# Loading x in 5 KB runs, attention by head halves, filter rows turned by VectorE, and loads paced by stores, in a gated mix of a long convolution and dilated attention

## The chip, the cores and the metric

One core of a Trainium2 chip. The metric is the time of one execution in device microseconds. With one core a run is called slow when it lies over 1.5% above the fastest of the same kernel. A ratio in this text is the mean time of one kernel's fast runs over that of the other's fast runs of the same rounds, so it is not quite the ratio of the medians that stand beside it.

## The reference, cut to what matters

S = 2048 tokens, D = 640 channels, bf16. Two branches are mixed by a gate per token.

```python
g = sigmoid((x * gate_w).sum(-1, keepdims=True))            # x is A_q
# a: short shift filter of k (4 taps), times v, then a long convolution, times q
kv = k_shift * v
y  = irfft(rfft(kv, 2*S) * rfft(ssm_k, 2*S))[:S] + kv * ssm_D
a  = x * y
# b: 32 heads of 20 channels; each token attends to 8 positions, 2 apart
q, k, v = x @ wqkv ;  b = softmax(q . k_gathered, masked) . v_gathered @ wo
return g * a + (1 - g) * b
```

## The kernel before

Tokens are worked on in 36 blocks of 57 queries and 64 keys, of even and odd tokens apart. x is loaded block by block (overlapping blocks, runs of one token row, 1.25 KB), transposed by TensorE, and a ScalarE copy writes each transposed block contiguously:

```python
def transposes(m):                                   # 18 times, two blocks each
    tr = ppv.tile([128, 8, 128], BF, name="trx", tag="trx")
    for dt in range(NDT):
        nc.tensor.transpose(tr[:, dt, :], xs(m)[:, 128*dt:128*dt+128], ident[:, :])
    nc.scalar.copy(xT[:, :, 128*m:128*m+128], tr[:, 0:NDT])
```

Then come the v projection (12 of 18 pairs of blocks; the other six during attention), the gate, and projections of q and k, whose rows are collected in a stage tile `stg` and sent by DMA into the score operands `kq`. Two stage tiles exist, so a projection waits until an earlier tile is sent. VectorE meanwhile makes the kv product. Attention is 24 steps: scores, exponential on ScalarE (`ET`), products with v (`O`), division on VectorE (`oS`). The output projection (`tr`, `oT`, `op`, `fin`, store to `b_scr`) of a third of the tokens runs among the steps of the next third. At the end of the eighth step all inputs of the convolution are asked for at once:

```python
if k == NT - 1:
    load_h(0)                                           # filter, runs of 128 bytes
    nc.sync.dma_start(G[:], ...)                        # constants, 2 MB
    for q in range(4):
        nc.sync.dma_start(kv[32*q:32*q+32], ...)        # 2.6 MB
    for g in range(1, NG):
        load_h(g)
```

The convolution follows: first transforms (`Am`), second (`Up`, `Hs`), inverse (`i`, `Cm`), by five groups of 16 channels, and a last inverse with the mixing and the stores.

The softmax here doesn't subtract the row's maximum and nothing guards it: scores larger than these inputs give would overflow.

Of the kernel before, what the change touches and what calls it, by code (L numbers as in the profile page):

```python
# [18 lines left out]
D = 640  # L19
# [10 lines left out]
PRE = 7  # L30
XW = 2 * NSB * KB
# [100 lines left out]
def kernel(  # L132
# [33 lines left out]
    Dz = p0.tile([128, 160], BF, name="Dz")  # L166
    g_nat = p0.tile([128, 16], F32, name="g_nat")
    omg = p0.tile([128, 16], F32, name="omg")

# [3 lines left out]
    xS = pA.tile([128, 4 * 2 * NSB * CB], BF, name="xS", tag="K0")  # L173
# [11 lines left out]
    pr = pB.tile([128, 4, 4 * D], BF, name="pr")  # L185
    v23 = pB.tile([128, 2, 4, D], BF, name="v23")
# [3 lines left out]

    def xs(m):
        return xS[:, m * D:(m + 1) * D]
# [5 lines left out]
    def load_x(m0, m1):  # L198
        for sub in range(2):
            for m in range(m0, m1):  # L200
                k0, k1 = (PRE if sub == 0 and m % 9 == 0 else 0), (KB - 2 if sub == 1 and m % 9 == 8 else KB)
                if (k0, k1) != (0, KB):
                    for i, n in split16(k1 - k0):
                        nc.sync.dma_start(xs(m)[KB * sub + k0 + i:KB * sub + k0 + i + n],
                                          raw(x2, xrow(2 * m + sub, k0 + i) * D, [[2 * D, n], [1, D]]))
            ms = [m for m in range(m0, m1) if not ((sub == 0 and m % 9 == 0) or (sub == 1 and m % 9 == 8))]
            a = ms[0]
            for b, nxt in zip(ms, ms[1:] + [-1]):
                if nxt != b + 1:
                    nc.sync.dma_start(xS[KB * sub:KB * sub + KB, a * D:(b + 1) * D].rearrange("p (m d) -> p m d", d=D),  # L210
                                      raw(x2, xrow(2 * a + sub, 0) * D, [[2 * D, KB], [4 * QB * D, b + 1 - a], [1, D]]))
                    a = nxt

    def load_w(w):
        nc.sync.dma_start(W[:, :, w, :], W3[:, :, w, :])

    kh = kvw[:, 0:19 * D].rearrange("p (t d) -> p t d", d=D)
    vns = [kvw[:, (19 + 4 * e) * D:(23 + 4 * e) * D].rearrange("p (t d) -> p t d", d=D) for e in range(2)] + [v23[:, 0], v23[:, 1]]

    def load_kv(c):  # L220
        if c == 0:
            nc.gpsimd.memset(kh[0:1, 0:3, :], 0.0)
            for p, n in ((1, 112), (113, 15)):
                nc.sync.dma_start(kh[p:p + n, 0:3, :], raw(k2, (16 * p - 3) * D, [[16 * D, n], [D, 3], [1, D]]))
        nc.sync.dma_start(kh[:, 3 + 4 * c:7 + 4 * c, :], raw(k2, 4 * c * D, [[16 * D, 128], [D, 4], [1, D]]))
        nc.sync.dma_start(vns[c], raw(v2, 4 * c * D, [[16 * D, 128], [D, 4], [1, D]]))

    nc.sync.dma_start(ident[:], ca["ident"].ap())
    for m in (0, 9):
        nc.gpsimd.memset(xs(m)[0:PRE], 0.0)  # L230
        nc.gpsimd.memset(xs(m + 8)[96:128], 0.0)
    load_x(0, 4); load_w(2); load_x(4, 9); load_x(9, 13)
# [3 lines left out]
    load_x(13, 18)  # L236
    load_kv(0)
    load_w(1); load_w(0)
    for c in range(1, 4):
        load_kv(c)  # L240
    nc.gpsimd.memset(Dz[:], 0.0)
    nc.gpsimd.tensor_copy(VW[:, :, :, DH], valid[:].unsqueeze(2).to_broadcast([128, 18, H]))
    for q in range(4):
        nc.gpsimd.dma_start(Dz[32 * q:32 * q + 1, :], A_ssm_D[160 * q:160 * q + 160].unsqueeze(0))
# [6 lines left out]
    def kv_gen():  # L251
        nc.vector.tensor_copy(wl[:], wraw[:].rearrange("p c j -> p j c"))
# [26 lines left out]
    def transposes(m):  # L279
        tr = ppv.tile([128, 8, 128], BF, name="trx", tag="trx")  # L280
        for dt in range(NDT):
            nc.tensor.transpose(tr[:, dt, :], xs(m)[:, 128 * dt:128 * dt + 128], ident[:, :])
        nc.scalar.copy(xT[:, :, 128 * m:128 * m + 128], tr[:, 0:NDT])

    def vproj_half(m, a, ps):
        for dt in range(NDT):
            nc.tensor.matmul(ps, lhsT=xT[:, dt, 128 * m:128 * m + 128], rhs=W[:, dt, 2, 320 * a:320 * a + 320],  # L287
                             start=(dt == 0), stop=(dt == NDT - 1))

    def vproj(m):  # L290
        ps = ppv.tile([128, 2, 512], F32, name="psv", tag="mm", bufs=3)
        for a in range(2):
            vproj_half(m, a, ps[:, a, 0:320])
        nc.scalar.copy(VW[:, m, :, 0:DH].rearrange("p (a h) d -> p a h d", a=2),
                       ps[:, :, 0:320].rearrange("p a (h d) -> p a h d", h=16))
# [38 lines left out]
    def feat_copies(e):  # L334
        for t in range(4):
            if e or t:
                for p in range(2):
                    ld.copy(kq[e][:, t, NSB * p:NSB * p + NSB], kq[0][:, 0, NSB * p:NSB * p + NSB], 800, eng="d")
                    ld.t["d"] += 600
                    yield  # L340
# [16 lines left out]
    def qk_send(ft, stg):  # L357
        for h in range(H):
# [10 lines left out]
    def qk_gen():  # L369
        for ft in range(NDT - 1):  # L370
            stg = new_stg()
            for c in range(5):
# [3 lines left out]
                for part in range(2):  # L376
                    qk_evac(stg, c, part, ps[:, part])
                if c < 4:
                    yield
            if ft == 2:  # L380
# [3 lines left out]
                for _ in feat_copies(1):  # L384
                    pass
            qk_send(ft, stg)
            yield

    def late_qk():
        stg = new_stg()  # L390
        for c in range(5):
            for part in range(2):
                ps = ppa.tile([128, 512], F32, name="pj2", tag="w", bufs=2)
                qk_part(NDT - 1, c, part, ps)
                qk_evac(stg, c, part, ps, eng="da"[part])
                if (c, part) == (4, 1):
                    qk_send(NDT - 1, stg)
                yield

    def late_v():  # L400
        for m in range(12, 18):
            for a in range(2):
                ps = ppa.tile([128, 512], F32, name="pv2", tag="w", bufs=2)
                vproj_half(m, a, ps[:, 0:320])
                ld.copy(VW[:, m, 16 * a:16 * a + 16, 0:DH], ps[:, 0:320].rearrange("p (h d) -> p h d", h=16), 320, eng="da"[a])
                yield
# [9 lines left out]
    def s1_gen(key, g):  # L416
        Am = p3.tile([128, 64, 4, IL], BF, name="Am", tag="Am", bufs=3)
        st[key] = Am
        for oc in range(4):
            ps = ps_tile("s1")  # L420
            psq = ps[:].rearrange("p a m -> p (a m)").rearrange("p (q l j) -> p q l j", q=4, l=4)
            for il in range(4):
                i = 4 * oc + il
                for qp in range(2):
                    rows = slice(64 * qp, 64 * qp + 64)
                    if key[0] == "h":
                        lhsT = h_lin[rows, IL * g + i].rearrange("p c n -> p (c n)")
                    else:
                        lhsT = kv[rows, :, :, IL * g + i].rearrange("p c n -> p (c n)")
                    nc.tensor.matmul(psq[:, 2 * qp:2 * qp + 2, il, :], lhsT=lhsT, rhs=F1b[rows, :], start=True, stop=True,  # L430
                                     tile_position=(64 * qp, 0), skip_group_check=True)
            ld.copy(Am[:, :, :, 4 * oc:4 * oc + 4], psq.rearrange("p q l j -> p j q l"), 1024)
# [56 lines left out]
    transposes(0)  # L489
    transposes(1)  # L490
    for m in range(12):
        vproj(m)
        transposes(m + 2)
        advance(kvg, 1)
    for m in range(14, 18):
        transposes(m)
    gate()
    feats(0)
    ld.t = dict(a=0.0, d=4000.0)
    qk = qk_gen(); fc = feat_copies(0)  # L500
    for k in range(20):
        advance(qk, 1)
        advance(kvg, 1)
        if k >= 3:
            advance(fc, 2)
        if k == 12:
            gate_end()
    while advance(kvg, 1):
        pass
# [6 lines left out]
    wo = pD.tile([128, NDT, D], BF, name="wo")  # L516
    nc.sync.dma_start(wo[:], B_wo.rearrange("(t p) n -> p t n", p=128))
# [8 lines left out]
    halves = [(gi, t, hf) for gi in range(NGI) for t in range(NT) for hf in range(2)]  # L526
# [48 lines left out]
    def op_tr(j):  # L575
# [4 lines left out]
        oT = pD.tile([128, NDT, 128], BF, name="oT", tag="oT", bufs=3)  # L580
# [11 lines left out]
    def op_half(j, hf):  # L592
# [8 lines left out]
        if hf == 1:  # L601
            op_store(j)

# [24 lines left out]
    def load_h(g):  # L628
        for q in range(4):
            for c in range(2):  # L630
                nc.gpsimd.dma_start(h_lin[32 * q:32 * q + 32, IL * g:IL * g + IL, c, :],  # L631
                                  raw(A_ssm_k, (160 * q + 80 * c + IL * g) * S, [[64, 32], [S, IL], [1, 64]]))

    def tap0(g):
        r = h_lin[:, IL * g:IL * g + IL, :, 0]
        nc.vector.tensor_tensor(r, r, Dz[:].rearrange("p (c i) -> p i c", c=2)[:, IL * g:IL * g + IL], ALU.add)

    opg = None
    lqk, lv = late_qk(), late_v()
    steps = [(gi, t) for gi in range(NGI) for t in range(NT)]  # L640
    scores(0)
    scores(1)
    for k in range(len(steps)):
        if k + 1 < len(steps):
            scores(2 * k + 2)
            scores(2 * k + 3)
        pv(2 * k)
        pv(2 * k + 1)
        gi, t = steps[k]
        if gi == 0:  # L650
            advance(lqk, (3, 3, 2, 2, 0, 0, 0, 0)[t])
            advance(lv, (0, 0, 1, 2, 3, 3, 3, 0)[t])
        if k == NT - 1:
            sC.close()
            pF = ctx.enter_context(tc.tile_pool(name="pF", bufs=1, side="left", reuse_waits="tile"))
            kv = pF.tile([128, 2, 64, 80], BF, name="kv")
            G = pF.tile([128, 32, 2, 128], BF, name="G")
            h_lin = pF.tile([128, 80, 2, 64], BF, name="h_lin", tag="hl")
            load_h(0)
            nc.sync.dma_start(G[:], cf["G"].ap().rearrange("p (a r b) -> p a r b", a=32, r=2))  # L660
            for q in range(4):
# [125 lines left out]
```

## Time and profile before

| | before |
|---|---|
| median of 3 runs | 337.01 us (336.86 to 339.55) |
| span of the profiled run, mean clock | 335.7 us, 0.813 |
| head (loads, projections, kv product) | to 98.5 |
| attention with output projection | to 208.5 |
| convolution up to the first inverse matmul | to 243.7 |
| other groups; last inverse and stores | to 310; to 335.7 |

The prediction shows the page, the chain and the windows. Of the groups (busy time, mean ns of one, idle time before), the copy of a transposed block:

```profile
L283 ACT COPY xT<-trx 128x640 bf16<-128x640 bf16 x18 | 12.1, 698 | 6.0 <-PE trx L282 6.0
```

And TensorE's waits in attention, 98.5 to 208.5 us (columns: total us, how often, longest; "issue" means that the profile shows nothing that was awaited; that TensorE then had no instruction is my reading, from the holes 128 matmuls apart and the 43 packets of 16 KB on the instruction queue, both in the prediction):

```profile
PE sc L539 <- issue: 8.9, 3, 5.4
...
PE O L561 <- issue: 4.9, 1, 4.9
...
PE sc L539 <- DMA kq<-stg: 1.9, 2, 1.0
...
PE tr L579 <- DVE fin L600: 0.5, 1, 0.5
```

Read it as a budget: with the 1.2 us of issue before `op`, 15 us of attention are, by that reading, waits for instructions, and waits for rows or for the store buffers are almost nothing.

### The profile page before, as it was taken

Reading aid. Unit: us, or ns where it says so; the run is one execution under the profiler, and the core shown is the slowest. Engines: PE = TensorE matmul, PEld = TensorE weight load, DVE = VectorE, ACT = ScalarE, POOL = GpSimd, SP = SyncE. Lnnn points to the kernel's source line nnn. Section 1 sums busy time; section 2 is a strip of 40 time slices with the busy share of each in tenths; the row PEclk is TensorE's granted clock in tenths of the full one; section 3 lists DMA queues with packets and bytes.
Section 4 is the critical chain, followed back from the end, with each engine's and each line's share of the span. In section 5 each row is a group of like instructions: output and inputs, shape, how many; then the busy total and the mean of one; then the engine's idle time right before and its main releaser. Section 6 shows DMA issues by size and latency. Waiting matters only on the chain.

```text
span 335.7 us, 12259 instructions
## 1 busy us (share of the span) xinstructions
PE 238.3 (71%) x5549; PEld 175.0 (52%) x5556; DVE 188.4 (56%) x279; ACT 168.8 (50%) x247; POOL 52.9 (16%) x81
## 2 busy tenths in 40 slices
PE   1399899969549978643969987536696969677330
PEld 1277545535315655432746765536595958676320
DVE  0106999099924433211545555524949697973982
ACT  1167845355304544321546632625749595963670
POOL 7700231000200006235930000000000000000132
PEclk9999999999757997555877999567778797985855
DMA  6999953655375235997531112995503131397065
GB/s 174 227 220 361 415 140 94 144 120 145 108 146 129 56 85 199 212 199 159 130 96 31 43 53 85 206 234 139 129 2 87 45 86 44 66 221 159 19 164 138
DMA packets 16017, 46.23 MB, mean 138 GB/s; under 512 B 3811, under 2 KB 10833, under 8 KB 13872
## 3 DMA queue, kind: packets, MB, share of 16 engines
q1 hardware_dynamic: 13196, 38.14, 46.5%
q0 software_dynamic: 2768, 7.32, 8.3%
q8 instruction: 43, 0.70, 0.9%
q14 instruction: 10, 0.07, 0.1%
HBM read 26.75 MB, written 7.87 MB: 103 GB/s over the span
## 4 chain that ended last, share of the span: by engine, by line
PE 35%; DVE 22%; DMA 13%; issue 12%; ACT 10%; SPq 5%; POOL 0%; DVEq 0%; ACTq 0%; POOLq 0%
PE i L482 8%; PE op L595 6%; DVE pr L256 6%; PE s L445 5%; DMA kq<-stg 5%; ACT Am L119 4%; PE O L561 3%; DVE pr L260 3%; PE sc L539 3%; DMA xS<-in_A_q_dram 3%; PE pj L349 3%; DMA kvw<-in_A_k_dram 3%; DVE kq L121 3%; SPq L363 2%; ACT Up L119 2%
## 5 line engine op out<-in xcount | busy, mean ns | idle before, releaser
L349 PE MATMUL pj<-xT,W 128*128 128x456 bf16 (+3 forms) x243 | 50.9, 366 | 8.4 <-ACT stg L119 7.7
L542 ACT ACTIVATE ET<-sc 128x684 bf16<-128x684 f32 x48 | 33.3, 740 | 30.9 <-PE sc L539 28.7
L349 PEld LDWEIGHTS <-W 128*128 128x128 bf16 x250 | 24.8, 101 | 32.8 <-issue 13.2
L119 ACT CAST stg<-pj 128x456 bf16<-128x456 f32 (+3 forms) x45 | 21.4, 531 | 35.0 <-PE pj L349 17.7
L445 PE MATMUL s<-Am,G 64*128 64x64 bf16 x1280 | 25.6, 201 | 15.9 <-issue 11.6
L631 POOL DMA_DIRECT2D h_lin<-in_A_ssm_k_dram x40 | 25.8, 650 | 56.0 <-PE sc L539 40.3
L482 PE MATMUL i<-M,Hs 128*128 128x128 bf16 x160 | 28.9, 276 | 6.4 <-DVE Hs L469 4.3
L445 PEld LDWEIGHTS <-G 64*128 64x128 bf16 x1280 | 23.7, 103 | 17.4 <-issue 15.6
L256 DVE TENSOR_TENSOR pr<-kvw,wl 128x2560 bf16<-128x2560 bf16 x16 | 22.9, 1487 | 16.9 <-DMA kvw<-in_A_k_dram 16.8
L119 ACT CAST Am<-s 128x1024 bf16<-128x1024 f32 x25 | 24.1, 1060 | 12.8 <-PE s L430 8.4
L755 POOL DMA_DIRECT2D out_dram<-qg x12 | 6.0, 502 | 154.6 <-DVE qg L753 154.6
L482 PE MATMUL i<-M,Hw 128*128 128x128 bf16 x160 | 28.6, 276 | 0.4 <-DVE Hw L469 0.4
L595 PE MATMUL op<-wo,oT 128*128 128x320 bf16 x120 | 25.4, 359 | 3.8 <-ACT oT L582 2.3
L539 PE MATMUL sc<-kq 31*64 31x57 bf16 x1152 | 16.9, 206 | 14.6 <-issue 8.9
L482 PEld LDWEIGHTS <-Hs 128*128 128x128 bf16 x160 | 24.1, 159 | 5.1 <-DVE Hs L469 4.7
L568 DVE RECIPROCAL rd<-O 128x24 f32<-128x24 f32 x24 | 7.4, 306 | 34.5 <-PE O L561 34.5
L287 PEld LDWEIGHTS <-xT 128*128 128x128 bf16 x180 | 18.3, 105 | 14.1 <-issue 5.7
L539 PEld LDWEIGHTS <-kq 31*64 31x64 bf16 x1152 | 13.3, 115 | 22.9 <-issue 19.6
L482 PEld LDWEIGHTS <-Hw 128*128 128x128 bf16 x160 | 23.8, 158 | 2.6 <-DVE Am L121 1.1
L287 PE MATMUL psv<-W,xT 128*128 128x320 bf16 x120 | 20.8, 326 | 5.1 <-DMA W<-in_B_wqkv_dram 5.1
L119 ACT CAST Cm<-i 128x1024 bf16<-128x1024 f32 x13 | 13.1, 1012 | 19.7 <-PE i L482 19.7
L582 ACT COPY oT<-tr 128x640 bf16<-128x640 bf16 x18 | 12.5, 692 | 20.0 <-PE tr L579 19.7
(69 smaller groups left out, 409.9 us busy)
## 6 DMA issues: line engine op xcount, KB each, us to landing
Hw<-Hs SPq DMA_DIRECT2D x10, 512.0 KB
kq<-stg SPq DMA_DIRECT2D x28, 170.2 KB
kvw<-in_A_k_dram SPq DMA_DIRECT2D x4, 640.0 KB
kv_scr<-kvo POOLq DMA_DIRECT2D x4, 640.0 KB, 5.5
kv<-kv_scr SPq DMA_DIRECT2D x4, 640.0 KB
h_lin<-in_A_ssm_k_dram POOLq DMA_DIRECT2D x40, 64.0 KB, 4.0
qg<-in_A_q_dram SPq DMA_DIRECT2D x4, 640.0 KB
bl<-b_scr SPq DMA_DIRECT2D x4, 640.0 KB
```

Of the source, the lines that this page charges most:

```text
L119: self.nc.scalar.copy(dst, src)
L121: self.nc.vector.tensor_copy(dst, src)
L256: nc.vector.tensor_tensor(pr[:, j].rearrange("p (n c) -> p n c", n=4), kh[:, 4 * c + 3 - j:4 * c + 7 - j, :], wl[:, j, :].unsqueeze(1).to_ ...
L287: nc.tensor.matmul(ps, lhsT=xT[:, dt, 128 * m:128 * m + 128], rhs=W[:, dt, 2, 320 * a:320 * a + 320], start=(dt == 0), stop=(dt == NDT - 1))
L349: nc.tensor.matmul(ps[:, 0:nb * wd], lhsT=W[:, dt, which, 128 * ft:128 * ft + 128], rhs=rhs, start=(dt == 0), stop=(dt == NDT - 1))
L445: nc.tensor.matmul(o, lhsT=G[rows, j, r, :], rhs=Am[rows, 2 * j + r, :, :], start=(r == 0), stop=(r == 1), tile_position=(64 * c, 0), skip ...
L482: nc.tensor.matmul(o, lhsT=src[:, c, :, :, 8 * oc + il].rearrange("p q j -> p (q j)"), rhs=M[:, k, :], start=(k == 0), stop=(k == 1), skip ...
L539: nc.tensor.matmul(sc[64 * sub:64 * sub + 64, hh, QB * mb:QB * mb + QB], lhsT=kqt[r:r + DH + NF, t % 4, si, 0:KB], rhs=kqt[r:r + DH + NF, ...
L542: nc.scalar.activation(ETs[i % NET][:, :, 0:NW], sc[:, :, 0:NW], ACT.Exp, scale=SCALE)
L582: nc.scalar.copy(oT[:], tr[:])
L595: nc.tensor.matmul(op[:, 0:320], lhsT=oTs[j][:, ft, :], rhs=wo[:, ft, 320 * hf:320 * hf + 320], start=(ft == 0), stop=(ft == NDT - 1))
L631: nc.gpsimd.dma_start(h_lin[32 * q:32 * q + 32, IL * g:IL * g + IL, c, :], raw(A_ssm_k, (160 * q + 80 * c + IL * g) * S, [[64, 32], [S, IL ...
```

## The change

Its intent: fewer and longer DMA runs for x, with the overlapping key blocks cut out on the chip; attention ordered by halves of the heads, so that half of the staged rows may be sent later; the filter loaded in 4 KB rows and turned by 20 VectorE transposes; kv and G cut in eight pieces, one behind each of the first stores of output rows, instead of a flood; and two groups of the filter's first transform moved into attention. All 18 pairs of blocks of the v projection now precede attention, and the transposed output rows (`oT`) get two buffers instead of three. The diff, cut to its core:

```diff
-    def load_x(m0, m1):  ... blocks of 64 rows, 1.25 KB runs
+    def load_x(c):
+        nc.sync.dma_start(xN[:, 4*c:4*c+4, :], raw(x2, 4*c*D, [[16*D, 128], [D, 4], [1, D]]))
...
+        dst = xTn[:, :, j % 2, PRE:PRE + S // 2].rearrange("p t (n u) -> p t n u", u=8)[:, :, :, j // 2]
+        ld.copy(dst, tr[:, 0:NDT], NDT * 128, eng="ad"[j % 2])
-        nc.scalar.copy(xT[:, :, 128 * m:128 * m + 128], tr[:, 0:NDT])
+    def windows(e, g):                     # 6 copies of 128 x 1920
+        nc.vector.tensor_copy(xT[...], src)
...
-            if ft == 2:                     # all 32 heads of a tile sent at once
+            if ft < NDT - 2:
+                qk_send(ft, stg, 0)         # first half of the heads
+            else:
+                feats(1) ... feature copies of the second tile
+                load_hn(0); load_hn(1)      # filter rows
+                qk_send(ft - 1, held[-2], 1)
+                qk_send(ft, stg, 1)
...
         if hf == 1:
             op_store(j)
+            if paced:
+                nc.sync.dma_start(*paced.pop(0))
...
+            nc.vector.transpose(hT[:, g]..., hns[g]...)
...
+    steps = ([(0, t) for t in range(4)] + [(1, t) for t in range(4)] + [(0, t) for t in range(4, 8)]
+             + [(1, t) for t in range(4, 8)] + [(2, t) for t in range(8)])
+    for k in range(8):
+        plan[k] = [("q", (1, 1, 1, 2)[k % 4])]          # late q/k projection
+    for k in range(4):
+        plan[12 + k] = [("o", 5 if k % 2 else 4)]       # output projection, first third
+    for k in range(8):
+        plan[16 + k] = [("p", 3 if k % 4 == 3 else 2), ("s", 1)]   # second third, filter
...
+        if k == 8:                          # was: before attention
+            wo = pF.tile([128, NDT, D], BF, name="wo"); nc.sync.dma_start(wo[:], ...)
```

The transposed tile j holds tokens 16p + j, so its columns belong at every eighth place of the natural order: `dst` steps by 8 elements, 16 bytes.

## The prediction

> **What bounds the kernel now.** I read the page first (busy shares, slices), then the windows of 10 us, then the chain of work, then the timeline where the chain shows holes. No engine is full: on the page
>
> ```profile
> PE 238.3 (71%) x5549; PEld 175.0 (52%) x5556; DVE 188.4 (56%) x279; ACT 168.8 (50%) x247; POOL 52.9 (16%) x81
> PEclk9999999999757997555877999567778797985855
> GB/s 174 227 220 361 415 140 94 144 120 145 108 146 129 56 85 199 212 199 159 130 96 31 43 53 85 206 234 139 129 2 87 45 86 44 66 221 159 19 164 138
> ```
>
> TensorE's 71% is inflated, because its granted clock falls to about half in several slices. So the kernel must be read by stage. From the timeline I take five: loads, projections and the kv product, to 98.5 us; attention with output projection, to 208.5 (110 us); convolution up to the first inverse matmul at 243.7 (35 us); the other groups, to 310 (66 us); the last inverse with stores, to 335.7 (26 us).
>
> The head ends on a chain (columns: start, duration, what):
>
> ```profile
> 84.92 1.49 DVE kvo L265
> 87.07 4.66 DVE kq L121 x7
> 91.81 0.72 DVE kq L121
> 93.25 4.65 DMA kq<-stg
> 97.91 0.55 ACT stg L119
> 98.50 2.29 PE pj L349 x5
> ```
>
> VectorE finishes the kv product, copies the feature rows of the second key/query tile, the staged rows are sent, and only then is a stage buffer free for the fifth projection. TensorE had issued the first scores at 83.65 and then lost some 10 us. VectorE, not TensorE, sets the end of the head.
>
> In attention and convolution the holes are of another kind (timeline, TensorE rows; the bracket is the idle time before the row and its releaser):
>
> ```profile
> 146.56 0.33 PE L539 MATMUL sc<-kq 31*64 31x57 bf16 x9 [5.43 <-issue]
> ...
> 155.50 0.66 PE L561 MATMUL O<-VW,ET 64*64 64x21 bf16 x35 [4.90 <-issue]
> ```
>
> ```profile
> 223.36 0.88 PE L445 MATMUL s<-Am,G 64*128 64x64 bf16 x26 [6.73 <-issue]
> ```
>
> "issue" says that no semaphore was awaited: TensorE had no instruction. Between the end of one hole and the start of the next I count 26+48+5+10+39 and 9+48+5+5+48+13 matmuls, 128 both times. The windows give the surroundings (busy of each engine, then clock, DMA share, GB/s):
>
> ```profile
> 140.00:150.00 10.00, 4.57 (x153) 2.98 (x152) 1.85 (x5) 2.17 (x3) 3.90 (x6) 0.50 1.01 198
> 150.00:160.00 10.00, 4.32 (x91) 2.87 (x74) 1.69 (x5) 2.06 (x3) 5.54 (x9) 0.50 0.77 160
> 160.00:170.00 10.00, 9.84 (x423) 7.37 (x422) 5.45 (x14) 6.02 (x10) 10.00 (x17) 0.87 0.54 137
> ```
>
> While the convolution's inputs (h, G, kv, all issued at once at 128 us) fill the DMA engines, TensorE does a third of the matmuls that it does once they are in, at half clock.
>
> [...] queue 8 moved 0.70 MB in 43 packets, 16 KB each, and 128 matmuls with 128 weight loads are 256 instructions. [...] the clock is halved [...]: 0.50 around the 5 us holes, and a projection matmul of 512 columns starts every 0.43 us after the wait at 90 us against 0.2 before. [...] the loads of 32 partitions run near 200 GB/s at full share, the 128-partition loads of 30 to 40 us at 401. [...] Here 2178 elements take 753 ns[...]; no row before has an odd block step like the new window copies.
>
> **The change, part by part.** Head, TensorE side. x (2.6 MB instead of 2.95, 5 KB runs instead of 1.25 KB) should come at the 400 GB/s of the k and v loads instead of 220: with the 0.64 MB of the shift kernel 3.3 MB / 400 = 8 us, so by 11.5 us. W for v (0.8 MB at 220 = 3.6 us) by 15. The 16 transposes (18 before) ping-pong on two PSUM buffers at about 0.72 us each and end near 14.5; the six window copies, 1920 elements each, 0.7 us by the copy row, run 14.5 to 19. The v projection needs only the first: it starts at about 15, all 18 blocks now (12 before). The cadence before is 1.52 us per block at full clock: 27.5 us, plus 2 for a cold start, to 44.5. Gate 4.6 us, to 49. Four q/k projections at 9.3 us each (first evictions 45.86 to 55.19): to 86.5, 3 us later than before. All their evictions are on ScalarE: ten a projection, 5.3 us in 9.3, hidden.
>
> Head, VectorE side. kv product: 16 products at 1.49, four adds at 2.82, eight short ops at 1.5, one cast: 48.6 us. It starts near 20 (28.3 before). But the feature copies now stand in the queue after 15 of its 25 steps, reached at about 46.5, while the feature rows are loaded only behind the gate's store and its four reloads: gate end 49, plus 8.5 us as before, 57.5. That wait eats 11 us; then 4.2 of copies, 20.4 of remaining product, 5.6 of copies for the second tile: 88 to 89. Then the short sends, some 5 us: 93. Head: 93 for 98.5, **-5.5**. The gain in load time is mostly spent in the wait for the features.
>
> Attention. The twelve late v half blocks (10.7 us of TensorE) are gone; the same 24 steps, nine further q/k units and 36 output units stay; 8 half units of the filter's first transform and 20 VectorE transposes come in. A step has 1.05 us of TensorE at full clock (0.50 scores, 0.49 products), 1.48 of ScalarE (2 x 0.74), 1.05 of VectorE. A transpose of 512 elements [...] is estimated at 0.7 us from the 1216 ns of a 1024-element eviction: 14 us in all beside some 45 of other VectorE work, hidden. By steps: seven with 1.3 q/k units of 1.03, 2.7 us each, 19; four bare at about 1.9, 8, plus 4 for the wait for the last heads' rows (nothing covers the sends now); four with 4.5 output units at 4.4, 17.6, plus 3 of slow fetch; eight with 2.25 output units and one filter unit at 3.5, 28; six full projections as before, 11. Sum 91 for 110, **-19**. What does it is that h comes in 4 KB rows from before attention on and the 4.6 MB of kv and G are cut into eight pieces, one behind each store: at any time about one piece of 3 us is in the way of an instruction block, not thirty.
>
> Convolution, first part. 35 us before, of which 6.7 + 2.0 holes, half clock (0.57) behind them, and the filter's transforms of two groups with the tap additions (about 4 us at the start, 3 later) go away. Left: 8 units in 6.5 us, the 8 with products in 8, the 8 of the next first transforms in 8 (236 to 244 now): 22.5, **-12.5**.
>
> Rest. The units are the same, 66 us. But qg and T (3.7 MB, about 200 GB/s: 18 us of full DMA) move from the first part into the first of these groups, which needs a block of instructions each 5.7 us (384 matmuls in 17 us). One hole as long as before goes with them: **+6**. The last 26 us are untouched.
>
> Sum: 93 + 91 + 22.5 + 72 + 26 = 304.5; the timed run is 1.3 longer than the span: **306 us**, 0.91 of before.
>
> **Rivals.** First: the head gets worse. For it: every window needs all of x, all 18 v blocks now precede attention, and the feature wait blocks VectorE in order. Scattered writes (a 16-byte step) could slow the transposes' evictions and the windows could run at 2 us. Against: TensorE's work is covered by VectorE's chain anyway. It would give a head of 104 and 317 us. Second: the flood is only displaced. 1.5 pieces a step of 4.4 us are 218 GB/s, as much as such loads draw; if the block fetch stays at 9 to 10 us, the output steps double (+15), and qg stops the convolution twice (+7): 325 us. Against: pacing limits itself, since a held TensorE makes no stores. Third: the holes' cost was even larger than I count, as the clock recovers everywhere; attention then nears its TensorE work, 25 + 9 + 24 + 4 + 10 = 72 us, and the moved flood hides behind evictions: 284 us.
>
> **Range and chances.** The three ends are 284, 317 and 325; none alone is likely in full, so 294 to 319 for eight in ten. Same needs more than 330, which takes the first two rivals together: 0.05. Slower 0.02, faster 0.93.
>
> **What would show it.** Right: TensorE's clock near 0.8 to 1.0 where it was 0.50; no issue hole above 3 us in attention; scores starting at 85 to 88 us and the steps flowing from about 93; VectorE waiting some 10 us for feature rows near 50; window copies near 0.7 us; the first inverse matmul near 207; one hole of 5 us or more after it, with DMA share near 1. Wrong: an attention stage over 105 us, or a head over 100, or a VectorE group of transposes over 25 us.

Of its figures, the 2 us for a cold start and the copy of 2178 elements are these in the trace before: the first two blocks of the v projection took 2.83 and 2.73 us where the later ones took 1.52, and the copy is VectorE's `kq<-kq`, 753 ns. The 0.7 us for a transpose is my estimate from the eviction named there.

## The result, and the profile after

Median 369.56 us of four runs (365.13 and 368.34 fast, 370.79 and 372.87 slow); the ratio of the fast runs is **1.092, 95% interval 1.074 to 1.109**. The kernel is slower, and the prediction was wrong in direction. The profiled run is a fast one with a span of 363.2 us and a clock of 0.827, against 335.7 and 0.813 before. The prediction had given "slower" a chance of 0.02.

| stage | before | predicted | after |
|---|---|---|---|
| head | 98.5 | 93 | 125.3 |
| attention with output projection | 110 | 91 | 116 |
| convolution, first part | 35 | 22.5 | 18.8 |
| other groups | 66 | 72 | 79.4 |
| last | 26 | 26 | 23.7 |

Two stages hold the miss: the head by 32 us and attention by 25.

**The head, at its start.** The groups of the same copy as above, now on two engines with a step of 16 bytes, and below them the two new VectorE groups:

```profile
L123 DVE COPY xTn<-trx 128x640 bf16<-128x640 bf16 x8 | 23.9, 2984 | 10.8 <-PE trx L270 10.8
...
L121 ACT COPY xTn<-trx 128x640 bf16<-128x640 bf16 x8 | 23.9, 2989 | 10.2 <-PE trx L270 10.2
...
L279 DVE COPY xT<-xTn 128x1920 bf16<-128x1920 bf16 x6 | 4.1, 754 | 0.1
```

The same 640 elements per partition take 2.99 us instead of 0.70. The profile's shape column is the same in both kernels; it does not show the step. The last such copy ends at 36.7 us, and the v projection starts at 37.6 where it started at 13.6 before.

**The head, at its end.** The chain, and SyncE's queue (start, duration):

```profile
109.74 8.04 DMA kq<-stg
117.78 4.75 issue
```

```profile
103.04 2.11 SPq L503 DMA_DIRECT2D hn<-in_A_ssm_k_dram  x2
106.52 16.28 SPq L352 DMA_DIRECT2D kq<-stg  x11
```

The sends of the second head half stand in one queue behind 1 MB of filter rows. The first eviction of the fifth projection, which needs a stage tile free, starts at 122.7.

**Attention.** TensorE's waits from 125.3 to 241.3 us:

```profile
PE sc L565 <- DMA kq<-stg: 10.1, 6, 5.8
PE s1e L435 <- DVE fin L626: 5.9, 1, 5.9
...
PE O L587 <- issue: 2.6, 2, 1.7
PE sc L565 <- issue: 1.7, 2, 1.2
```

The waits for instructions fell from 15 us to 4.3, as the prediction had it. In their place stand 10.1 us for staged rows (1.9 before) and 5.9 for the store buffers. The clock tells the same: adding up windows of 1 us (with a window of clock under 0.75 counted as half), attention before was 23.0 us without a matmul, 32.3 busy at half clock and 54.7 at full; after, 29.4, 35.4 and 51.2.

**The other groups.** The flood of qg and T, moved here, costs what a flood costs; one window (busy of PE, PEld, DVE, ACT, POOL, then clock, DMA share, GB/s):

```profile
260.00:270.00 10.00, 7.56 (x145) 7.35 (x143) 6.95 (x7) 4.05 (x4) 0.00 (x0) 0.74 1.00 211
```

TensorE waits for instructions 3.3 us in the convolution's first part (8.8 before) and 14.6 in the other groups, 260.1 to 339.5 us (2.9 before).

### The profile page after: what moved, and what is told of

Its sections match the earlier page's. It is cut to its first block, busy times and chain, and to the rows that moved or that the text cites. A ratio compares the mean times of both kernels' runs of the same rounds, so it can differ in the third digit from the quotient of the medians.

```text
span 363.2 us, 12172 instructions
## 1 busy us (share of the span) xinstructions
PE 248.3 (68%) x5546; PEld 178.4 (49%) x5546; DVE 234.1 (64%) x315; ACT 182.3 (50%) x240; POOL 23.9 (7%) x39
## 4 chain that ended last, share of the span: by engine, by line
PE 39%; DMA 17%; DVE 15%; ACT 12%; issue 11%; SPq 4%; POOL 0%; ACTq 0%; DVEq 0%; POOLq 0%
PE i L491 8%; PE psv L285 8%; PE op L621 6%; ACT Am L121 5%; DMA kq<-stg 4%; DMA kvw<-in_A_v_dram 4%; DMA b_scr<-fin 4%; PE s L454 3%; DMA xN<-in_A_q_dram 3%; PE O L587 3%; SPq L352 2%; DVE pr L244 2%; PE pj L338 2%; PE sc L565 2%; ACT Up L121 2%
## 5 line engine op out<-in xcount | busy, mean ns | idle before, releaser
L338 PE MATMUL pj<-xT,W 128*128 128x512 bf16 (+3 forms) x250 | 51.9, 364 | 1.7 <-ACT stg L121 1.7
L454 PE MATMUL s<-Am,G 64*128 64x64 bf16 x1280 | 23.6, 194 | 19.4 <-issue 17.9
L121 ACT CAST stg<-pj 128x456 bf16<-128x456 f32 (+3 forms) x45 | 21.2, 534 | 29.7 <-DMA kq<-stg 17.3
L338 PEld LDWEIGHTS <-W 128*128 128x128 bf16 x250 | 23.9, 99 | 24.5 <-issue 5.1
L454 PEld LDWEIGHTS <-G 64*128 64x128 bf16 x1280 | 21.7, 98 | 21.0 <-issue 20.6
L123 DVE COPY xTn<-trx 128x640 bf16<-128x640 bf16 x8 | 23.9, 2984 | 10.8 <-PE trx L270 10.8
L285 PE MATMUL psv<-W,xT 128*128 128x320 bf16 x180 | 27.4, 320 | 4.0 <-DVE xT L279 4.0
L121 ACT COPY xTn<-trx 128x640 bf16<-128x640 bf16 x8 | 23.9, 2989 | 10.2 <-PE trx L270 10.2
L565 PE MATMUL sc<-kq 31*64 31x57 bf16 x1152 | 19.2, 213 | 13.0 <-DMA kq<-stg 10.1
L121 ACT CAST Hs<-s 128x1024 bf16<-128x1024 f32 x19 | 19.0, 1022 | 14.7 <-PE s L454 14.5
L270 PE MATMUL trx<-ident,xN 128*128 128x128 bf16 x80 | 9.8, 304 | 23.8 <-ACT xTn L121 12.7
L626 DVE CAST fin<-op 128x320 bf16<-128x320 f32 x24 | 11.6, 486 | 22.0 <-PE op L621 14.2
L587 PE MATMUL O<-VW,ET 64*64 64x21 bf16 x1152 | 18.6, 189 | 10.0 <-DVE oS L597 7.3
L478 DVE TENSOR_TENSOR Hs<-Up,Hs 128x1024 bf16<-128x1024 bf16 x20 | 13.8, 690 | 17.7 <-ACT Up L121 10.9
```

Source lines behind the costliest of these rows:

```text
L121: self.nc.scalar.copy(dst, src)
L123: self.nc.vector.tensor_copy(dst, src)
L285: nc.tensor.matmul(ps[:, a, 0:320], lhsT=xT[:, dt, 128 * m:128 * m + 128], rhs=W[:, dt, 2, 320 * a:320 * a + 320], start=(dt == 0), stop=( ...
L338: nc.tensor.matmul(ps[:, 0:nb * wd], lhsT=W[:, dt, which, 128 * ft:128 * ft + 128], rhs=rhs, start=(dt == 0), stop=(dt == NDT - 1))
L454: nc.tensor.matmul(o, lhsT=G[rows, j, r, :], rhs=Am[rows, 2 * j + r, :, :], start=(r == 0), stop=(r == 1), tile_position=(64 * c, 0), skip ...
L478: nc.vector.tensor_tensor(blk_(H_), blk_(Up), blk_(H_), ALU.mult)
```

## The experiments

Each ran beside the kernel before on the same chip. All results passed the check. So did e11 and e15, which leave out the filter, or kv and G: the check says little about the convolution's part of the output. To compare ratios in time, 1 per cent is 3.35 us. The ratio of the change alone has an interval of 5.8 us to either side, so a difference to it is no finer than that.

By medians of all runs, slow ones too, the ratios are: the change 1.097; e1 1.042, e4 1.062, e5 1.031, e6 1.031, e7 1.030, e8 1.038, e9 1.006, e10 0.999, e11 1.015, e12 1.015, e13 1.004, e14 1.001, e15 1.002, e16 1.002, e17 0.980, e18 0.990. The profiled runs of e1, e5, e6, e7, e15 and e18 are slow ones; for the waits of e5 and e7 a fast trace is named beside them.

### e1: x in short runs again, contiguous copies

```diff
-nc.sync.dma_start(xN[:, 4*c:4*c+4, :], raw(x2, 4*c*D, [[16*D, 128], [D, 4], [1, D]]))
+nc.sync.dma_start(xN[:, 4*c:4*c+4, :]..., raw(x2, 512*c*D, [[2*D, 128], [256*D, 2], [1, 2*D]]))
-dst = xTn[...].rearrange("p t (n u) -> p t n u", u=8)[:, :, :, j // 2]
+dst = xTn[:, :, j % 2, PRE + 128*(j//2) : PRE + 128*(j//2) + 128]
```

> The changed kernel with one thing altered: x is loaded in runs of 2.5 KB so that a transposed tile's 128 columns lie next to each other in the x tile, and its eviction writes whole rows instead of every eighth element. Theory (the scattered eviction, 2.98 us a tile against 0.70 in the kernel before, holds TensorE, VectorE and ScalarE back together): the eviction falls to about 0.7 us on ScalarE and 0.7 to 0.8 on VectorE, the last transpose ends near 15 us instead of 36, the first v projection starts at 15 to 17 instead of 37.6, and everything behind it moves up by about 21 us: some 345 us. Rival (the head is set by VectorE's chain and the wait for feature rows, or by the loads, and the evictions are hidden beside them): the evictions get short but the time falls by less than 8 us.

Ratio 1.039 (1.029 to 1.049), median 349.25 us; against 1.092 that is some 17.6 us. The copies take

```profile
L121 ACT COPY xTn<-trx 128x640 bf16<-128x640 bf16 x8 | 5.7, 708 | 12.3 <-PE trx L271 12.3
```

(708 ns in the fast traces of e9 and e13 too) and the v projection starts at 21.3 us instead of 37.6, later than the 15 to 17 expected, though x now comes in runs of 2.5 KB. So the 5 KB runs did not pay for their step.

### e2: all scattered copies on ScalarE

```diff
-eng="ad"[j % 2]
+eng="a"
```

> The changed kernel with all 16 scattered evictions on ScalarE, none on VectorE. If each scattered write has a fixed cost, whoever makes it: still about 2.98 us each, 16 in a row, 48 us, and the v projection starts near 60 us. If the 2.98 us come from two engines writing at once and getting in each other's way: about 1.0 to 1.5 us each and the v projection starts before 37 us.

One look: 381.61 us; a copy takes 2.99 to 3.36 us. The v projection starts at 52.8 us. It is no collision of two engines; a single engine is as slow by itself (2.99 us on ScalarE, 2.98 on VectorE in e3).

### e3: a ladder of destination steps

At the end of the changed kernel, copies of 640 elements from PSUM with various steps, on both engines.

> The changed kernel with a row of copies of 640 bf16 elements added behind the last store, on ScalarE and on VectorE one after the other: destination step 2, 4, 8, 16, 32 bytes from PSUM, runs of 2 and of 4 elements every 16 bytes, then SBUF to SBUF with a scattered destination and with a scattered source, at last both engines at once. Theory of a fixed cost of a write to a new place: steps of 2 and 4 bytes near 0.7 us, a jump at some step up to about 2.98, the same on both engines, runs of 4 shorter in proportion to the number of runs, and the scattered source much cheaper than the scattered destination. Rival (PSUM reads or the collision of engines cause it): alone every step takes about 0.7 to 0.9 us, and only the last pair takes 2.98. The output stays right.

Timeline of ScalarE, each line the first of a pair: steps of 2, 4, 8, 16 and 32 bytes, and last runs of two elements (4 bytes) every 16 bytes:

```profile
354.88 0.69 ACT L805 COPY kv<-pb 128x640 bf16<-128x640 bf16 x1
...
356.33 0.87 ACT L805 COPY kv<-pb 128x640 bf16<-128x640 bf16 x1
...
358.13 1.57 ACT L805 COPY kv<-pb 128x640 bf16<-128x640 bf16 x1
...
361.34 2.99 ACT L805 COPY kv<-pb 128x640 bf16<-128x640 bf16 x1
...
367.38 2.83 ACT L805 COPY kv<-pb 128x640 bf16<-128x640 bf16 x1
...
373.10 0.72 ACT L808 COPY kv<-pb 128x640 bf16<-128x640 bf16 x1
```

VectorE shows 0.49, 0.87, 1.57, 2.98, 2.83 and 0.72. Lone 2-byte writes grow slow with their step up to 16 bytes; pairs at the same step cost 0.03 us on ScalarE and 0.23 on VectorE, runs of four nothing (0.69 and 0.49). From SBUF instead of PSUM the scattered destination took 3.02 us on ScalarE but 1.58 on VectorE, so on VectorE the source has a part in it; a scattered source with a contiguous destination took 1.31 and 0.72. The last pairs, meant to run on both engines at once, ran one after the other; only e2 speaks on a collision.

### e4: filter rows sent for after the staged rows

```diff
-                load_hn(0); load_hn(1)
                 qk_send(ft - 1, held[-2], 1)
                 qk_send(ft, stg, 1)
+                load_hn(0); load_hn(1)
```

> The changed kernel with the first two filter loads (0.5 MB each) issued after the sends of the staged key and query rows instead of ahead of them on the same queue. Theory (the sends, 16 us from 106.5 to 122.8, wait behind the filter loads and for room on the queue): the sends take about 10 us and the fifth projection's first eviction comes 5 to 6 us earlier, near 117; 360 us. Rival (the sends are slow by themselves, or the kv store on the other queue slows them): the same time within 2 us.

Ratio 1.0575 (1.048 to 1.067), some 11.4 us. The first eviction of the fifth projection starts at 115.2 instead of 122.7. The direction is the theory's, and so about is the size (some 10 us were expected, 5 to 6 of them at this spot); 7.5 us of it is seen at this spot.

### e5, e6, e7: the fixes stacked

e5 is e1 and e4 together. e6 adds the first tile's features right behind the transposes; e7 adds an earlier late projection:

```diff
     for j in range(16):
         transposes(j)
+    feats(0)                                   # e6
-        plan[k] = [("q", (1, 1, 1, 2)[k % 4])]
+        plan[k] = [("q", (2, 2, 2, 2, 2, 0, 0, 0)[k])]     # e7
```

> The changed kernel with x loaded in short runs and contiguous evictions (as e1) and with the two filter loads behind the staged sends (as e4). Theory (two independent losses: 18 to 20 us of scattered evictions, 7 to 12 us of sends queued behind the filter loads): the gains add, 369 - 20 - 13 = 336, that is 1.00 of the kernel before, from 0.99 to 1.02. Rival (e4's gain beyond the 7.5 us seen at its spot was noise or cancels against e1's earlier head, which also brings the sends forward): 343 or more, 1.02 to 1.04.

> As e5, with the first tile's feature rows loaded right behind the transposes instead of behind the gate. Theory (VectorE's queue stands 11 us at the feature copies and VectorE ends the head): the wait goes, the head then ends on TensorE's projections, scores start at about the same 91 us but the fifth projection's first eviction, 97 in e5, comes some 6 us earlier, and the time falls by 5 to 10 us, to 0.97 to 0.99 of before. Rival (the head is bound by TensorE once the evictions are contiguous): no change within 2 us of e5.

> As e6, with the ten late projection units taken two a step from the first step on, so that the last heads' rows leave three steps earlier. Theory (TensorE stands some 13 us before the ninth step for rows whose sends left too late): that wait falls to 3 us or less and the time by 6 to 10 us, to 0.94 to 0.97 of before. Rival (fuller steps at the start take what the earlier sends give): within 2 us of e6.

e5: one of four runs fast, 336.39 us against a mean of 334.9 before (1.004): the two losses add, 17.6 + 11.4 = 29 us. By the medians (345.29 against 369.56) it is 24 us. e6: 1.0156 (1.010 to 1.022), no gain, though VectorE's wait for the features (9.7 us in e5's trace) is gone. e7: one fast run, 337.1 us (1.007); the waits for staged rows (10.1 us in e5, 10.5 in e4's fast trace) are gone from TensorE's list, in e9's fast trace too. Both theories fail in the time. In e7 other waits have come up at the same place:

```profile
120.34 0.57 PE L566 MATMUL sc<-kq 31*64 31x57 bf16 x32 [3.00 <-issue]
...
128.90 0.20 PE L566 MATMUL sc<-kq 31*64 31x57 bf16 x1 [6.17 <-issue]
...
168.23 0.58 PE L436 MATMUL s1e<-F1b,hT 64*128 64x128 bf16 x7 [5.27 <-DVE fin L627]
```

The last rows, a filter group and the output weights, 1.9 MB, now share the time around 120 us. I take them to hold the instructions: in e13, without the weights' 0.8 MB there, the longest issue wait in attention is 2.1 us. e9's fast trace has the same two holes, 3.3 and 6.2 us. What e6 did comes under e18.

### e8: pacing undone

All eight pieces at the ninth step, on top of e7.

> As e7, with pacing undone: the eight pieces of kv and G are all issued at the ninth step, ahead of the output projection, none behind a store. Theory (a piece of 8 us in front of each store is what makes the output steps wait for the staging of the output rows): the waits for the store, 7 us each at most, some 10 us in all, go; a flood of 18 us or more stands in bare steps, where it slows one block fetch or two: 3 to 8 us faster than e7. Rival (the pacing is what saves attention from block fetches at 9 us): holes of 5 us come back at the ninth to twelfth steps and it is 3 to 10 us slower than e7.

1.027 (1.022 to 1.032). The rival is right: behind the pieces, which are issued from 122.7 us on, stand holes of 8.95 and 7.0 us with the releaser issue, and issue waits in attention are 25.6 us against 12.2 in e7. A third hole, 3.9 us, ends at 110.7 and so lies before them. In this order of steps pacing seems worth having; e7, against which this is said, has one fast run, and by medians the two are 2.7 us apart.

### e9, e10: what pacing itself does

e9 takes e7 and issues the pieces from ScalarE's queue (`nc.scalar.dma_start`), so that no store stands behind a piece in SyncE's. e10 is the kernel before with one part of the change, kv and G in eight pieces behind the stores.

> As e7 (337 us in its fast runs, 335 before), with the eight pieces of kv and G issued by ScalarE on its own queue, at the same places of the order, instead of behind the stores on SyncE's. Theory (the stores stand in line behind a piece in one queue, 5 and 8.5 us in e7, and the filter stage then waits 5.3 us for the eviction into the output rows): the wait of the filter stage for that eviction falls below 1.5 us, and the time by 5 to 9 us, to 0.97 to 0.99 of before. Rival (the stores are slow because the DMA engines are full, whatever the queue): the waits stay within 2 us of e7's and the time within 3 us.

> The kernel before with one part of the change alone: kv and G cut in eight pieces, one behind each of the first stores; the filter stays where it was. Theory (pacing takes away holes of instruction fetch, 15 us of issue waits in attention, and gives some of it back as waits for stores): issue waits in attention fall from 15 to 8 us or less, as the filter's 2.6 MB still come at once; the time falls by 3 to 8 us, 0.975 to 0.99. Rival (pacing gives back all that it takes): within 1 per cent of before, with waits for stores of 5 us or more in attention.

e9: 1.007 (0.998 to 1.016), as e7. The filter stage's wait for the stores went (5.3 us in e7), as the theory had it, but not the time: a wait moved to ScalarE, 5.0 us for `oT` in e9 and 10.3 in e12, which has the same queue. By changing the queue that issues the piece nothing is won. In e12, ScalarE's queue at that place (start, duration) shows the issue itself held:

```profile
156.76 12.42 ACTq L631 DMA_DIRECT2D G<-cf_G  x2
```

e10: 0.998 (0.990 to 1.006), no gain: 12.3 us of issue waits instead of 15, and TensorE without a matmul for 22.2 us instead of 23.0. By itself, pacing of these 4.6 MB does nothing for the kernel before, while the filter's 2.6 MB still come at once.

### e11: without the VectorE transposes (wrong)

> As e7, wrong on purpose: the 20 transposes of VectorE are left out and the filter is all zero. Theory (they lie beside other work, as the prediction had it, and do not set the end): 0 to 3 us faster than e7. Rival (at 1.05 us each in the one VectorE queue they hold back the division of each attention step, and so TensorE): 10 us or more faster, with the waits of the products for VectorE, 3.1 us in e7, gone and the steps of four bare units shorter.

GpSimd clears the filter's tile instead, 8.6 us in the head. 1.017 (1.008 to 1.026); four fast runs, mean 341.8 us, not faster than e7's 337.1; by medians it is 1.015 against 1.030, some 5 us faster. The rival, 10 us or more, falls: 20 transposes at 1.05 us (512 elements per partition each) lie beside other work.

### e12: the loads for the end spread

> As e9, and the loads for the end (four pieces of qg and T, 3.7 MB at once behind the second filter group in e7) spread: two pieces there, two a group later, T another group later. Theory (these loads slow the fetch of instructions: issue waits of some 4 us at 240 and 248 us in e7): one of the two waits goes and the time is 3 to 6 us below e9. Rival (each smaller flood costs a hole of its own): within 2 us of e9.

1.006 (0.997 to 1.015) against e9's 1.007; issue waits from 208.5 to 310 us are 17.4 us in seven holes against 17.2 in six. The rival is right: each smaller flood costs a hole.

### e13, e14, e15: what holds attention

e13 loads the output weights in the head, into the place of the v weights (dead by then). e14 also leaves the fifth and sixth store without a piece. e15 is e13 without loading kv and G at all (zeros, wrong).

```diff
-    W = pC.tile([128, NDT, 3, D], BF, name="W")
+    W = pC.tile([128, NDT, 2, D], BF, name="W")
+    Wv = p0.tile([128, NDT, D], BF, name="Wv", tag="wv")
...
+    wo = p0.tile([128, NDT, D], BF, name="wo", tag="wv")
+    nc.sync.dma_start(wo[:], ...)               # ahead of the q/k projections
```

> As e7, with the output weights loaded in the head instead of at the ninth step: they take the place of the v weights, which are dead after the v projection. Theory (at the ninth step the last rows, a filter group and the output weights, 1.9 MB together, hold the instruction blocks of TensorE: holes of 3.0 and 6.2 us in e7): with 0.8 MB less there, one hole of about 3 us stays, the ninth and tenth steps take 8 instead of 13 us, and the time falls by 4 to 8 us, below the kernel before. Rival (the rows themselves, in short runs, are what holds the fetch): holes of 8 us or more stay and the time is within 2 us of e7.

> As e13, and no piece of G behind the fifth and sixth store; the four come behind the seventh to tenth. Theory (a piece and the last filter group, 1 MB together, are in front of the stores at the eighteenth step: its 10 us in e7): the longest wait for an eviction into the output rows falls from 5.3 to under 2 us and the eighteenth step from 10 to 5 or less: 4 to 6 us faster than e13. Rival (whatever comes there in its place meets the same stores): a wait of 4 us or more turns up a few steps later and the time is within 2 us of e13.

> As e13, wrong on purpose: kv and G are not loaded, GpSimd writes zeros, so attention has none of these 4.6 MB. Theory (the mixed steps at full clock take the predicted 3.5 to 4 us, and the rest of their 44 us is waiting behind the pieces and the half clock that follows): the last eight steps take 28 to 33 us and the time is 8 to 14 us below e13. Rival (the mixed steps are limited by their own chain of two shared buffers, not by loads): they stay above 38 us and the time is within 4 us of e13.

e13: 0.994 (0.985 to 1.003). The longest issue wait in attention falls from 6.2 to 2.1 us, as the theory has it; its fast trace, beside the 6.2 us of e9's:

```profile
PE sc L569 <- issue: 5.1, 4, 2.1
```

e14: 0.990 (0.981 to 0.998), not clear of e13; the longest wait for the store buffers falls from 5.8 to 2.8 us, where under 2 was expected. (The step is the seventeenth, not the eighteenth, counting from one.) e15: 0.983 (0.972 to 0.994), only some 3.7 us below e13 where 8 to 14 were expected, within the intervals of the two. GpSimd's clearing of kv and G, 15.6 us in attention, is in these times. Its profiled run is a slow one, so its times are not compared; but its windows say why bytes are not the whole story:

```profile
160.00:170.00 10.00, 9.35 (x206) 5.89 (x204) 6.84 (x13) 5.15 (x9) 0.00 (x0) 0.50 0.07 20
170.00:180.00 10.00, 9.83 (x222) 5.99 (x224) 5.42 (x13) 3.39 (x6) 0.00 (x0) 0.50 0.12 33
180.00:190.00 10.00, 9.20 (x230) 6.13 (x227) 7.30 (x15) 5.62 (x9) 0.00 (x0) 0.50 0.06 16
```

With DMA share near 0.1 and TensorE busy over 92% (by the modelled ends of its matmuls), the clock stays at 0.50 for these 30 us, and five `op` matmuls take 1.5 us where they took 0.85 just before. It fell at a wait for the store buffers of 2.3 us, at 156 to 158 us, behind one of 1.25 us for `oT`. Nothing in the profile says why it does not come back; after another hole, in e14, it came back behind some 20 us.

### e16, e17: the order of the units

e16 moves one output unit from the seventeenth step to the last, so that the third eviction into two buffers comes later. e17 also takes four of the eight filter units in the bare steps. The diff shows a second difference: e16 puts the filter unit of a mixed step ahead of its output units, e17 behind them again, as in e14.

```diff
-        plan[16 + k] = [("p", 3 if k % 4 == 3 else 2), ("s", 1)]
+        plan[16 + k] = [("s", 1), ("p", (1, 2, 2, 3, 2, 2, 2, 4)[k])]                          # e16
+        plan[16 + k] = [("p", (1, 2, 2, 3, 2, 2, 2, 4)[k])] + [("s", 1)] * (2 <= k < 6)        # e17
+    for k in range(8, 12):
+        plan[k] = [("s", 1)]                                                                   # e17
```

> As e14, with one output unit less at the seventeenth step (it moves to the last), so that the third eviction into two output-row buffers, which waits 4.4 us for a store there, comes a step later. Theory (that wait leaves a hole of 2.8 us on TensorE and some 20 us at half clock behind it): the wait is below 1 us, the half clock from 164 to 182 us is gone or short, and the time falls by 4 to 9 us, to 0.96 to 0.98 of before. Rival (the clock stays low from the sends at 114 us on, or drops at any small hole): within 2 us of e14, 0.99.

> As e16, and the four filter units of the first group taken in the four bare steps nine to twelve, the four of the second in steps nineteen to twenty-two. Theory (bare steps leave TensorE idle half the time at half clock, and the mixed steps are crowded): the mixed steps take 4 us less, the bare ones 2 more, and the clock comes back earlier: 2 to 5 us faster than e16. Rival (TensorE's work is the same and the bare steps are held by the sends): the same as e16 within 2 us.

e16: 1.005 (0.999 to 1.011), no better than e14. The wait for the store buffers fell to 1.0 us at most, but a hole of 3.3 us with the releaser issue opened there, and the clock fell all the same. The last step of attention still began 1.5 us earlier than in e14's trace; what follows it, which the edit does not touch, took 142.4 us against 136.3. **e17: 0.969 (0.962 to 0.976)**, three fast runs of 322.5 to 327.2 us, and faster than before by medians too (329.21 against 335.78). Counting 48 product matmuls to a step, e17's bare steps nine to twelve take 15.5 us with four filter units where e16's take 15.0 without: the units cost 0.5 us there. Steps 17 to 23 take 29.7 us instead of 33.9; the first products of the seventeenth and of the last step, in e16 and in e17:

```profile
157.50 0.57 PE L591 MATMUL O<-VW,ET 64*64 64x21 bf16 x48
...
191.40 0.37 PE L591 MATMUL O<-VW,ET 64*64 64x21 bf16 x24
```

```profile
150.92 0.57 PE L591 MATMUL O<-VW,ET 64*64 64x21 bf16 x48
...
180.60 0.37 PE L591 MATMUL O<-VW,ET 64*64 64x21 bf16 x24
```

The units' order inside a step is no better rival by the traces: e14, with e17's order, took 36.0 us for these steps. From the first product to that of the last step e17 takes 90.2 us, e16 94.7. Of the 13.3 us between their spans, these 4.5 lie where the edit is; 6.3 are earlier, in a head that the edit does not touch, and 2.5 behind attention.

### e18: why that head was shorter

The v weights are asked for ahead of the second half of x.

> As e17, with the v weights sent for between the second and third quarter of x instead of behind all of it. In the traces of e7 to e16 TensorE waits 4.5 us before the v projection (start 23.6 to 24.5), though the first window copy is done near 20.5, and the clock is at half behind it; in e17's, 1.5 us (start 20.4). Theory (the wait is for the weights' arrival, which differs from run to run, and some of e17's 11 us over e16 is that): the v projection starts at 20 to 21.5 in the trace, and the time is 0 to 3 us below e17's, with less spread, 0.96 to 0.97 of before. Rival (the wait is for the window copies, or e17's speed was the luck of its chip): start at 23 us or later, and 0.98 or more.

One fast run of six, 321.84 us (0.968 of the mean of before's fast runs, 332.6); the others 330.0 to 332.6; medians 331.03 against 334.55. The profiled run (330.79) has e17's order of units and a head 1.1 us later than e16's; its span is still 4.9 us shorter than e16's. It is a slow run, so this is only a hint of what the units' place gives alone. The v projection starts at 25.6 us, so the theory falls: the wait is not for the weights. The traces had the answer. The six window copies of e16, shortest, median and longest in ns, and GpSimd's timeline there:

```profile
L281 DVE COPY xT<-xTn x6: 745/745/3767, 19.8 to 26.1; 128x1920 bf16<-128x1920 bf16 x6
```

```profile
19.20 3.73 POOL L324 MEMSET kq<- 128x4356 bf16 x1 [0.69 <-PE trx L272]
```

And of e17:

```profile
L281 DVE COPY xT<-xTn x6: 745/746/4364, 19.5 to 26.5; 128x1920 bf16<-128x1920 bf16 x6
```

```profile
20.23 3.75 POOL L324 MEMSET kq<- 128x4356 bf16 x1
```

The early features of e6 brought GpSimd's clearing of the key/query tile, 3.7 us, beside the first window copy, which then ends 0.6 us behind it. The one copy beside the memset takes 3.77 us (4.36 in e17), the median of the six is 0.75; by what means a memset holds a copy, the traces do not show. In e5, where no memset runs there, all six take 0.75 to 0.77 us and the v projection starts at 21.4. In e17 the memset came 1 us later, the second copy paid, and TensorE started the v projection at 20.4 us instead of 23.6, and without the half clock behind (24.8 us instead of 27.2 for the projection). So e6 took away one wait and made another; that this is all of e6's missing gain is not shown, and a kernel with the memset elsewhere was not run.

## Why the prediction was wrong, point by point

**Transposes' evictions at 0.72 us (head, TensorE side): wrong, the largest miss.** They took 2.99 us, and the v projection started at 37.6 instead of 15. e1 and e3 show the cause, lone 2-byte writes 16 bytes apart. The prediction named this as its first rival and set it aside with "TensorE's work is covered by VectorE's chain anyway". That step was wrong in kind: the kv product was made to stand in the same VectorE queue behind the scattered copies, the windows and the feature wait, so a late start moved both chains. The rival's own size, windows at 2 us, was also wrong; they took 0.754.

**"Then the short sends, some 5 us": wrong.** They took 16.3 us. The prediction counted the sends by themselves and not what stands ahead of them in the queue, 1 MB of filter rows in the lines just above. e4 undoes it for 11.4 us.

**The feature wait of 11 us on VectorE: right** (11.3 in the trace), as were the window copies (0.754 us for 0.7).

**Attention 91: wrong by 25, in two terms.** By starts of the steps, the first (six of them, 124.4 to 142.1, 2.94 us each for 2.7) and the four output steps (21.7 for 20.6) are near. The four bare steps took 24.2 us where 8 + 4 stood: the wait for the last heads' rows was mis-sized, and e7 shows that without it the output weights and the filter group take its place. Seven of the eight mixed steps took 37 us where 7 x 3.5 = 24.5 stood. "At any time one piece of 3 us in the way" looked at the instruction blocks, where it is right, and not at the store, which must free one of two buffers: 5.9 us in one wait, and half clock behind it. The step of 3.5 us held only at full clock: the last full ones took 3.2 to 4.1.

**What does it is "that h comes in 4 KB rows ... and kv and G are cut": half right.** Waits for instructions did fall, 15 to 4.3 us. But e10 shows no gain from cutting kv and G in the kernel before, and e15 that what comes back without these bytes, 3.7 us, is not clear of the noise. The rest of my 19 us was the assumption that a hole removed gives back its length and the clock behind it. In e6, e7, e9 and e16 a wait removed was followed by another, and in e14 and e15 one of 2 to 3 us, shortly behind one of 1.3, was followed by half clock for 20 us and more.

**Convolution, first part, 22.5:** 18.8, better than said. **Rest, 72:** 79.4; one moved hole was counted, and 14.6 us of issue waits came; e12 shows that spreading the loads does not help. **VectorE's transposes beside other work: right** (e11), at 1.05 us instead of the estimated 0.7.

The ends of two rivals do not follow from their parts: 306 + 15 + 7 is 328, not 325, and 306 - 19 - 6 is 281, not 284. Nothing in the account hangs on it.

Together: 32.3 + 25 - 3.7 + 7.4 - 2.3 = 58.7 us, the distance of the spans, 363.2 - 304.5. Of this the two head losses are shown (29 us by e1, e4 and e5's one fast run, 24 by e5's median). The attention's 25 are shown in part: the output weights (e13) and the units' place (e17) bring the stack to 0.969 by fast runs and 0.980 by medians. Not settled: why the clock stays low as long as it does, and how much of e17's gain is the earlier head of its run, which by the traces goes with the moment at which a memset starts, and so is luck and not the edit's.

## What to carry to other kernels

A longer DMA run that left the scattering to an engine's copy only moved the cost here, and made it larger: keep the fastest step of a copy's destination contiguous (640 bf16 from PSUM by ScalarE: 0.69 us, against 2.99 at a step of 16 bytes), or write at least pairs of bf16 (0.72). When a transfer is moved or paced, read the whole queue around its new place: what stands behind it (a send, a store that frees one of two buffers, the next instruction block) paid for it here (16.3 us for the sends, 5.9 for the store buffers, 6.2 for the longest hole in e7), and in e6, e7, e9 and e16 a wait removed gave no gain while another followed. Put independent units into the steps whose engines stand idle before pacing anything: in e17 four units that cost 0.5 us in bare steps left the crowded ones 4.2 us shorter.
